# An output product by seven products instead of eight for some pairs of tiles, and gates made in steps

## The chip, the cores and the metric

The kernel runs on one core of one Trainium2 chip. The metric is the device time of one launch in microseconds (us), as the median of several runs. Its engines are named as in the profile: PE multiplies matrices (PEld is its weight load, which runs beside it), DVE and POOL are the vector engines, ACT computes functions, copies and casts, and SP issues the DMAs. Each engine works through its own queue in order, and waits for others by semaphores.

## The reference

Attention of 8 batches, 8 heads, 576 positions and 64 dimensions with two kinds of sparse mask (local for four heads, strided for the others) makes `x`, 4608 tokens by 512. Behind it stands a layer with a gate, which is the part that matters here:

```python
h = x @ w_in            # 4608 x 512 by 512 x 2048
g = h * np.cos(h)       # the gate, elementwise
return (g @ w_out)      # 4608 x 2048 by 2048 x 512
```

Inputs and output are float32 (the weights float64, converted on the chip).

## The kernel before

The program has two stretches. In the first, a loop over slots written out by hand (56 slots for each of the 8 batches, lines 716 to 735) lays the attention of one batch under the input product `x @ w_in` of the one before. That product is made by Strassen's seven products already, with 288 columns to a matmul (line 511), and its result goes to DRAM as `h_all`, 16 tiles ("f tiles") of 128 rows of h by 4608 tokens. In the last batch no attention is left; there `w_out` is read back as float32 (`both`, line 572) and split in two parts for the second stretch, and the first three gates are made.

All products are taken with operands split in two: `split` (line 158) makes a high part by a cast to the type fp32r on ACT (line 159) and a low part as the difference on POOL (line 160). A product is then three matmuls: high by high, high by low, low by high.

The second stretch is the output product `g @ w_out`, lines 739 to 747. It runs over 9 blocks `s` of 512 tokens (`TB`), and in each over the 16 f tiles. For each (s, f), `gate` makes g and `outer` multiplies:

- `gate` (lines 580 to 595) loads 128x512 of h, finds on ACT the whole number of turns k (line 585), subtracts them on DVE (586), takes the sine of the sum with a quarter turn on ACT (587), multiplies by h on DVE (591) and splits (594). The tile `r`, of which there are two, holds k, the rest, the sine and the product in turn; there are four of `g_hi` and `g_lo`. A gate is issued whole, `LAG` = 3 tiles ahead of its use.
- `outer` (lines 597 to 611) runs, for each of four groups of 128 tokens, three matmuls with 128x128 of g as the weight and 128x512 of w_out as the moving operand, into a PSUM bank that collects all 16 f tiles. At the last f tile the bank is copied out, on ACT and DVE in turn, and stored. Eight banks, two for each group, are in use.

The order of instructions on an engine comes from a scheduler that plays the program through with costs of its own. `in_turn` (line 122) keeps the matmuls in the order written, and `with_product` (line 131) keeps an operation from being placed ahead of the matmul that stands before it in the program; neither makes an engine wait.

PSUM has 8 banks; one holds 512 float32 columns. Pools of tiles (`tc.tile_pool`) give out a buffer again once its last reader is done.

Of the kernel before, what the change touches and what calls it, by code (L numbers as in the profile page):

```python
# [25 lines left out]
NTOK = B * S  # L26
P = 128
# [23 lines left out]
NFC = DFF // P  # L51
NF = NFC // 2
# [6 lines left out]
STEP = 7  # L59
# [4 lines left out]
PER_BATCH = NF * STEP  # L64
# [7 lines left out]
PROLOGUE = ((0,), (1,), (2,), (3,), (0, 4), (1, 0, 5), (2, 1, 6), (3, 2), (4, 4), (3,), (5, 5), (6, 6))  # L72
BUSY = (9, 2, 2, 2, 2, 2, 2, 10)

TB = 512
NTB = NTOK // TB
NTT = TB // P
LAG = 3
WG = 3


@with_exitstack
def attention_cos_ffn(ctx, tc, qkl, vl, qkvs, w_in, w_out, eye, eye16, mask_l0, mask_l, mask_s, out):
    nc = tc.nc
# [11 lines left out]
    quarter = const.tile([P, 1], F32, name="quarter")  # L96
# [6 lines left out]
    h_all = dram.tile([NFC, P, NTOK], F32, name="h_all")  # L103
    w_all = dram.tile([NFC, P, DM], F32, name="w_all")
# [26 lines left out]
    def with_product(begun):  # L131
        if turn is not None:
            order(begun, turn, "with this product")
# [21 lines left out]
            out=out, in0=top, scalar=3, in1=bits, op0=ALU.logical_shift_left, op1=ALU.bitwise_or  # L155
        )

    def split(x, hi, lo):
        with_product(nc.scalar.copy(out=hi, in_=x))  # L159
        nc.gpsimd.tensor_tensor(out=lo, in0=x, in1=hi.bitcast(F32), op=ALU.subtract)  # L160

    wi, whole = [], []

# [39 lines left out]
    class Attention:  # L203
        def __init__(self, stack):
            self.plain = True
            self.ld, self.wk = (
                stack.enter_context(tc.tile_pool(name=name, bufs=bufs, side="right", reuse_waits="tile"))
                for name, bufs in (("ld", 3), ("wk", 2))
            )
            self.sm = stack.enter_context(tc.tile_pool(name="sm", bufs=3, side="right"))  # L210
            pn_s.extend(self.wk.tile([P, SU, GP], F32, name=f"pn_s{i}", bufs=1) for i in range(2))
            for t in pn_s:
                nc.gpsimd.memset(t, 0.0)
            self.pn_s = itertools.cycle(pn_s)
            self.kept, self.spare, self.x = None, None, {}
# [349 lines left out]
    def output_weights(n):  # L565
        if n % WG:
            t = wp.tile([P, 2, 2, 2 * P], F32R, name="w", bufs=2 * NF).rearrange("p l m n -> p l (m n)")
        else:
            t = wp.tile([P, 2, 3, 2 * P], F32R, name="v").rearrange("p l m n -> p (l m n)")
            t = t[:, :2 * DM].rearrange("p (l n) -> p l n", l=2)  # L570
        both = more.tile([P, DM], F32, name="both")
# [6 lines left out]
    wo, pend = [], []  # L578

    def gate(s, f):  # L580
        h = hp.tile([P, TB], F32, name="h_in")
        nc.sync.dma_start(out=h, in_=h_all[f, :, s * TB:(s + 1) * TB])
        r = rp.tile([P, TB], F32, name="r")
        k = r.bitcast(I32)
        with_product(nc.scalar.activation(out=k, in_=h, func=AF.Copy, scale=1.0 / (2.0 * math.pi), bias=0.25))  # L585
        nc.vector.scalar_tensor_tensor(out=r, in0=k, scalar=-2.0 * math.pi, in1=h, op0=ALU.mult, op1=ALU.add)  # L586
        sin = nc.scalar.activation(out=r, in_=r, func=AF.Sin, bias=quarter)  # L587
# [3 lines left out]
        nc.vector.tensor_tensor(out=r, in0=r, in1=h, op=ALU.mult)  # L591
        g_hi = gp.tile([P, TB], F32R, name="g_hi")
        g_lo = gp.tile([P, TB], F32R, name="g_lo")
        split(r, g_hi, g_lo)
        return g_hi, g_lo

    def outer(s, f, g_hi, g_lo, acc):
        wh, wl = wo[f]
        for t in range(NTT):
            at = slice(t * P, (t + 1) * P)  # L600
            for i, (g, w) in enumerate(((g_hi, wh), (g_hi, wl), (g_lo, wh))):
                in_turn(nc.tensor.matmul(  # L602
                    acc[t], g[:, at], w, start=(f == 0 and i == 0), stop=(f == NFC - 1 and i == 2)
                ))
            if f == NFC - 1:
                o = op.tile([P, DM], F32, name="o")
                if t % 2:
                    nc.vector.tensor_copy(out=o, in_=acc[t])
                else:
                    nc.scalar.copy(out=o, in_=acc[t])  # L610
                nc.sync.dma_start(out=out[s * TB + t * P:s * TB + (t + 1) * P, :], in_=o)

    wp = ctx.enter_context(tc.tile_pool(name="wp", bufs=NF, reuse_waits="tile"))
    with ExitStack() as phase:
        cv = phase.enter_context(tc.tile_pool(name="cv", bufs=1))
# [8 lines left out]
        pools = banks  # L626
# [7 lines left out]
        m, n, o = ((pools[name], name) for name in "mno")  # L634
        acc = [(ps, f"acc{i}") for i in range(3)]
# [80 lines left out]
        for slot in range(max(plan) + 1):  # L716
            b, at = divmod(slot, PER_BATCH)
            if slot in plan:
                plan[slot]()
            for many, new in bursts.get(slot, ()):  # L720
                burst(many, new)
            for unit in turns.get(slot, ()):
                next(unit)
            for step in steps.get(slot, ()):
                step()
            if b == B - 1:
                if at == 0:
                    attention.close()
# [4 lines left out]
                    more = phase.enter_context(tc.tile_pool(name="more", bufs=WG, side="right", reuse_waits="tile"))  # L733
                if at >= PER_BATCH - 2 * STEP and at % 4 == 0 and len(pend) < LAG:
                    pend.append(gate(0, len(pend)))

    op = ctx.enter_context(tc.tile_pool(name="op", bufs=4, reuse_waits="tile"))
    ps_o = ctx.enter_context(tc.tile_pool(name="ps_o", bufs=2, space=bass.MemoryType.PSUM, reuse_waits="tile"))  # L740
    tiles = [(s, f) for s in range(NTB) for f in range(NFC)]
    for i, (s, f) in enumerate(tiles):
        if f == 0:
            acc = [ps_o.tile([P, DM], F32, name=f"acc{t}") for t in range(NTT)]
        if i + LAG < len(tiles):
            pend.append(gate(*tiles[i + LAG]))
        outer(s, f, *pend.pop(0), acc)


_OUT = ((NTOK, DM), "float32")  # L750
# [92 lines left out]
```

## Time and profile before

| | us |
|---|---|
| median of three runs | 884.25 (882.93 to 885.15) |
| the profiled run | 883.67 |
| its span, first to last instruction | 881.9 |
| input product and attention, up to the first output matmul | about 486 |
| output product, first to last matmul | 391.70 |
| from there to the end | 3.7 |

A row of the groups by line gives line, engine, operation, output and inputs by name, and the shape with the count; then the busy time and the mean of one in ns; then the idle time of the engine just before them, and what ended it. A row of the chain gives start, length and what ran. A row of the windows gives the stretch, its length, for PE, PEld, DVE, ACT and POOL the busy time with the number of instructions, then the granted clock of PE, the DMA share and GB/s. A row of the timeline gives start, length, engine, line, operation and tiles, and in brackets how long the engine was idle before it and who ended that.

### The profile page before, as it was taken

The numbers are of one execution on the slowest core, as the hardware profiler recorded it, in microseconds if no ns is written. First come the engines' busy times: TensorE is split into PE (matmuls) and PEld (weight loads), VectorE is DVE, ScalarE is ACT, GpSimd is POOL, SyncE is SP. The second block draws the span as 40 slices with busy tenths as digits, with TensorE's granted clock in tenths as the row PEclk, the third lists the DMA queues.
The fourth block names the chain that finished last, engine by engine and source line by source line (L and its number), as shares of the span: only waits on it lengthen the run. The fifth ranks groups of instructions, "written<-read, shape, count | busy, mean of one in ns | idle before, by whom it ended". The sixth has DMA issues, their size and how long they took to land.

```text
span 881.9 us, 21351 instructions
## 1 busy us (share of the span) xinstructions
PE 869.3 (99%) x8439; PEld 775.9 (88%) x8439; DVE 562.3 (64%) x966; ACT 530.1 (60%) x1020; POOL 398.2 (45%) x341
## 2 busy tenths in 40 slices
PE   8999999999999999999999999999999999999998
PEld 5799899999999999999999888888888888888886
DVE  5778655767576675676425666666666666666662
ACT  3776544435445463454457777777777777777772
POOL 2578974316024051151355444444444444444442
PEclk9999999999999999999999999999999999999999
DMA  9697444565556556643285434343434344444431
GB/s 333 206 294 259 141 147 158 196 220 191 195 188 234 198 196 201 197 159 122 101 278 188 135 96 144 100 145 101 144 100 141 112 129 120 128 119 121 131 109 48
DMA packets 70516, 143.83 MB, mean 163 GB/s; under 512 B 8208, under 2 KB 15632, under 8 KB 70416
## 3 DMA queue, kind: packets, MB, share of 16 engines
q1 hardware_dynamic: 69696, 142.24, 50.2%
q8 instruction: 66, 1.08, 0.5%
q14 instruction: 34, 0.28, 0.1%
q10 hardware_dynamic: 720, 0.23, 0.1%
HBM read 91.06 MB, written 51.38 MB: 162 GB/s over the span
## 4 chain that ended last, share of the span: by engine, by line
PE 52%; DMA 2%; ACT 1%; POOL 1%; DVE 0%; issue 0%; POOLq 0%; ACTq 0%
PE acc L602 44%; PE m L511 4%; PE n L511 2%; DMA both<-w_all 2%; PE o L511 1%; POOL w L160 1%; PE acc L312 0%; PE acc L377 0%; ACT w L159 0%; ACT r L585 0%; DVE r L586 0%; PE acc L294 0%; ACT r L587 0%; ACT L587 0%; PE acc L364 0%
## 5 line engine op out<-in xcount | busy, mean ns | idle before, releaser
L160 POOL TENSOR_TENSOR g_lo<-r,g_hi 128x512 fp32r<-128x512 f32 x144 | 186.3, 1294 | 205.2 <-ACT g_hi L159 201.0
L602 PE MATMUL acc<-w,g_hi 128*128 128x512 f32 x720 | 221.6, 389 | 0.0
L591 DVE TENSOR_TENSOR r<-r,h_in 128x512 f32<-128x512 f32 x144 | 151.0, 1049 | 103.9 <-ACT r L587 103.6
L602 PEld LDWEIGHTS acc<-w,g_hi 128*128 128x128 f32 x720 | 135.2, 188 | 28.1
L602 PE MATMUL acc<-w,g_lo 128*128 128x512 f32 x360 | 140.0, 389 | 0.0
L585 ACT ACTIVATE r<-h_in 128x512 int32<-128x512 f32 x144 | 91.1, 633 | 77.0 <-POOL g_lo L160 76.3
L602 PE MATMUL acc<-v,g_hi 128*128 128x512 f32 x432 | 133.0, 389 | 0.0
L587 ACT ACTIVATE r<-r,quarter 128x512 f32<-128x512 f32 x144 | 104.4, 725 | 23.1 <-DVE r L586 22.9
L586 DVE SCALAR_TENSOR_TENSOR r<-r,h_in 128x512 f32<-128x512 int32 x144 | 101.7, 707 | 22.4 <-ACT r L585 11.1
L511 PE MATMUL m<-x_hi,w 128*128 128x288 f32 x448 | 109.8, 300 | 1.9 <-DVE h L529 1.5
L511 PE MATMUL m<-x_hi,v 128*128 128x288 f32 x448 | 109.1, 298 | 1.0 <-ACT m L519 0.9
L602 PEld LDWEIGHTS acc<-v,g_hi 128*128 128x128 f32 x432 | 81.0, 188 | 16.8
L159 ACT CAST g_hi<-r 128x512 fp32r<-128x512 f32 x144 | 89.6, 623 | 2.4 <-PE acc L602 1.2
L602 PE MATMUL acc<-v,g_lo 128*128 128x512 f32 x216 | 84.0, 389 | 0.0
L511 PEld LDWEIGHTS m<-x_hi,w 128*128 128x128 f32 x448 | 78.0, 188 | 3.8 <-DVE h L529 2.2
L511 PEld LDWEIGHTS m<-x_hi,v 128*128 128x128 f32 x448 | 78.0, 188 | 2.5 <-ACT m L519 1.7
L602 PEld LDWEIGHTS acc<-w,g_lo 128*128 128x128 f32 x360 | 67.5, 188 | 14.0
L519 ACT COPY m<-m 128x288 f32<-128x288 f32 x112 | 44.5, 397 | 57.3 <-PE m L511 52.3
L511 PE MATMUL m<-x_lo,w 128*128 128x288 f32 x224 | 66.1, 295 | 0.0
L511 PE MATMUL m<-x_lo,v 128*128 128x288 f32 x224 | 66.1, 295 | 0.0
L264 POOL TENSOR_TENSOR pn_s<-e_sb,z 128x324 f32<-128x324 f32 x28 | 21.2, 756 | 93.3 <-DVE z L262 72.2
L264 POOL TENSOR_TENSOR e_sb<-e_sb,z 128x384 f32<-128x384 f32 x24 | 20.9, 872 | 92.1 <-DVE z L262 81.6
(115 smaller groups left out, 1704.5 us busy)
## 6 DMA issues: line engine op xcount, KB each, us to landing
h_all<-h SPq DMA_DIRECT2D x128, 288.0 KB, 2.7
h_in<-h_all SPq DMA_DIRECT2D x144, 256.0 KB, 2.7
out<-o SPq DMA_DIRECT2D x36, 256.0 KB, 2.4
qk<-in_qkvs SPq DMA_DIRECT2D x28, 324.0 KB, 4.0
qk<-in_qkl SPq DMA_DIRECT2D x21, 416.0 KB, 3.9
raw<-in_w_in SPq DMA_DIRECT2D x16, 512.0 KB, 4.7
raw<-in_w_out SPq DMA_DIRECT2D x16, 512.0 KB, 4.3
v<-in_vl SPq DMA_DIRECT2D x24, 224.0 KB, 3.1
```

The lines of the kernel that those rows point to most:

```text
L159: with_product(nc.scalar.copy(out=hi, in_=x))
L160: nc.gpsimd.tensor_tensor(out=lo, in0=x, in1=hi.bitcast(F32), op=ALU.subtract)
L264: nc.gpsimd.tensor_tensor(out=pn, in0=e, in1=z[:, :n].unsqueeze(2).broadcast_to([P, n, w]), op=ALU.mult)
L511: in_turn(nc.tensor.matmul(bank, a[:, c * P:(c + 1) * P], y[:, c], start=first and i == 0, stop=i == len(ops) - 1, skip_group_check=True,))
L519: nc.scalar.copy(out=t, in_=self.bank[name[0]])
L585: with_product(nc.scalar.activation(out=k, in_=h, func=AF.Copy, scale=1.0 / (2.0 * math.pi), bias=0.25))
L586: nc.vector.scalar_tensor_tensor(out=r, in0=k, scalar=-2.0 * math.pi, in1=h, op0=ALU.mult, op1=ALU.add)
L587: sin = nc.scalar.activation(out=r, in_=r, func=AF.Sin, bias=quarter)
L591: nc.vector.tensor_tensor(out=r, in0=r, in1=h, op=ALU.mult)
L602: in_turn(nc.tensor.matmul(acc[t], g[:, at], w, start=(f == 0 and i == 0), stop=(f == NFC - 1 and i == 2)))
```

## The change

The output product now runs over 18 blocks of 256 tokens (`TB = 2 * P`) and in each over 8 pairs of f tiles. A pair is a product of 2 by 2 blocks: two groups of 128 tokens by two f tiles, times two f tiles by two halves (256 columns) of w_out. For the pairs 1, 3 and 5 (`SEVEN`) of the 16 inner blocks it is made by Strassen's seven products, in the form with seven sums on either side; the other pairs, and all pairs of the first and last block, are plain, 12 matmuls of 512 columns as before. A product by seven has 256 columns. Both kinds add into the banks `lower` and `upper` (one for each group of tokens, three in rotation); four quarters of the two banks `more` collect the products that go to more than one place, which DVE adds up (`shared`) and puts on top in `store`.

The gate goes in four steps, issued 6, 4, 3 and 2 pairs ahead (`LEADS`): load; turns and their subtraction; sine and product (with the sums of a seven gate, on POOL); split. The sine goes to a PSUM tile (`wave`, three banks). The sums of w_out for the pairs by seven, and the cast of most of w_out, are made on DVE in the last batch; the last four f tiles of w_out are split in the output product.

```diff
-TB = 512
+TB = 2 * P
 NTB = NTOK // TB
-NTT = TB // P
-LAG = 3
-WG = 3
+SEVEN = (1, 3, 5)
+LEADS = (6, 4, 3, 2)
+AHEAD = tuple(PER_BATCH - n for n in (20, 17, 13, 10, 7, 3))
+BY_VECTOR = (2, 4)
+SUMMED = (14, 28, 35)
+LATE = 4
+OUTPUTS = (
+    (0, "b11", "more", 0), (2, "b21", "upper", 0), (6, "b22", "upper", 1), (1, 3, "lower", 0), (5, 2, "more", 1),
+    (3, 0, "more", 2), (4, 1, "more", 3),
+)
...
-    def split(x, hi, lo):
-        with_product(nc.scalar.copy(out=hi, in_=x))
-        nc.gpsimd.tensor_tensor(out=lo, in0=x, in1=hi.bitcast(F32), op=ALU.subtract)
+    def split(x, hi, lo, cast=nc.scalar.copy, rest=nc.gpsimd):
+        with_product(cast(out=hi, in_=x))
+        rest.tensor_tensor(out=lo, in0=x, in1=hi.bitcast(F32), op=ALU.subtract)
...
-        split(both, t[:, 0], t[:, 1])
+        split(both, t[:, 0], t[:, 1], nc.vector.tensor_copy)
...
+    def output_sums(cv, n):
+        f = SEVEN[n]
+        both = whole_tile(cv).rearrange("p (f n) -> p f n", f=2)
+        nc.sync.dma_start(out=both, in_=w_all[2 * f:2 * f + 2].rearrange("f p n -> p f n"))
...
+        first = nc.vector.tensor_tensor(
+            out=t[:, :2], in0=b[:, 1:2].broadcast_to([P, 2, 2 * P]), in1=b[:, 0:4:3], op=ALU.subtract
+        )
+        nc.vector.tensor_tensor(out=t[:, 2], in0=b[:, 3], in1=t[:, 0], op=ALU.subtract)
+        nc.vector.tensor_tensor(out=t[:, 3], in0=b[:, 2], in1=t[:, 2], op=ALU.subtract)
...
+        split(t[:, :3], most[:, 0], most[:, 1], nc.vector.tensor_copy)
...
+        split(t[:, 3], *last, nc.vector.tensor_copy)
...
     def gate(s, f):
+        h = hp.tile([P, 2 * TB], F32, name="h_in")
+        nc.sync.dma_start(
+            out=h.rearrange("p (f t) -> p f t", f=2),
+            in_=h_all[2 * f:2 * f + 2, :, s * TB:(s + 1) * TB].rearrange("f p t -> p f t"),
+        )
+        yield
...
+        yield
+        wave = sg.tile([P, 2 * TB], F32, name="wave")
+        sin = nc.scalar.activation(out=wave, in_=r, func=AF.Sin, bias=quarter)
...
+        pool = nc.gpsimd
+        if not seven(s, f):
+            low, pool = (wave, nc.vector) if f in BY_VECTOR else (r, nc.gpsimd)
+            nc.vector.tensor_tensor(out=low, in0=wave, in1=h, op=ALU.mult)
+            yield
+            g_hi, g_lo = (gp.tile([P, 7 * P], F32R, name=name) for name in ("g_hi", "g_lo"))
+            split(low, g_hi[:, :4 * P], g_lo[:, :4 * P], rest=pool)
+            gates[s, f] = g_hi, g_lo
+            yield
+        g = gs.tile([P, 8, P], F32, name="g")
+        nc.vector.tensor_tensor(out=g[:, :4].rearrange("p n t -> p (n t)"), in0=wave, in1=h, op=ALU.mult)
+        pool.tensor_tensor(out=g[:, 4], in0=g[:, 0], in1=g[:, 2], op=ALU.add)
+        pool.tensor_tensor(
+            out=g[:, 5:7], in0=g[:, 0:5:4], in1=g[:, 1:2].broadcast_to([P, 2, P]), op=ALU.subtract
+        )
+        pool.tensor_tensor(out=g[:, 7], in0=g[:, 3], in1=g[:, 6], op=ALU.subtract)
+        yield
+        g_hi, g_lo = (gp.tile([P, 7 * P], F32R, name=name) for name in ("g_hi", "g_lo"))
+        split(g[:, 1:].rearrange("p n t -> p (n t)"), g_hi, g_lo)
...
+        def pair(self, f, g_hi, g_lo):
+            (b1h, b1l), (b2h, b2l) = wo[2 * f:2 * f + 2]
+            if not seven(self.s, f):
+                for half, name in enumerate(("lower", "upper")):
+                    for n, (wh, wl) in enumerate(((b1h, b1l), (b2h, b2l))):
+                        gh, gl = (g[:, (2 * n + half) * P:(2 * n + half + 1) * P] for g in (g_hi, g_lo))
+                        self.add(name, 0, 2, ((gh, wh), (gh, wl), (gl, wh)))
+                return
...
+            for n, w, name, at in OUTPUTS:
+                wh, wl = plain[w] if w in plain else sums[f][w]
+                gh, gl = (g[:, n * P:(n + 1) * P] for g in (g_hi, g_lo))
+                self.add(name, at, at + 1, ((gh, wh), (gh, wl), (gl, wh)))
+        def shared(self):
+            more = self.banks["more"]
+            self.t = op.tile([P, 5, 2 * P], F32, name="t")
+            with_product(nc.scalar.copy(out=self.t[:, 0], in_=more[:, 0]))
+            nc.vector.tensor_tensor(out=self.t[:, 4], in0=more[:, 1], in1=self.t[:, 0], op=ALU.add)
+            yield
+            nc.vector.tensor_tensor(
+                out=self.t[:, 1:3], in0=more[:, 2:4], in1=self.t[:, 4:5].broadcast_to([P, 2, 2 * P]), op=ALU.add
+            )
+            nc.vector.tensor_tensor(out=self.t[:, 3], in0=more[:, 2], in1=self.t[:, 2], op=ALU.add)
+            yield
+        def store(self):
...
+                if "more" in self.banks:
+                    nc.vector.tensor_tensor(
+                        out=o, in0=self.banks[name], in1=self.t[:, 2 - 2 * half:4 - 2 * half], op=ALU.add
+                    )
+                elif half:
+                    nc.vector.tensor_copy(out=o, in_=self.banks[name])
+                else:
+                    nc.scalar.copy(out=o, in_=self.banks[name])
...
+                    sg = ctx.enter_context(tc.tile_pool(
+                        name="sg", bufs=3, space=bass.MemoryType.PSUM, side="right", reuse_waits="tile"
+                    ))
-                        for name, bufs in (("gp", LAG + 1), ("hp", 4), ("rp", 2))
+                        for name, bufs in (("gp", 3), ("hp", 5), ("rp", 3))
...
+    gs = ctx.enter_context(tc.tile_pool(name="gs", bufs=3, reuse_waits="tile"))
+    pools = {
+        name: ctx.enter_context(
+            tc.tile_pool(name=f"ps_{bufs}", bufs=bufs, space=bass.MemoryType.PSUM, reuse_waits="tile")
+        ) for name, bufs in (("lower", 3), ("more", 1))
+    }
+    pools["upper"] = pools["lower"]
...
+        ahead(i)
+        for step in made.get(i, ()):
+            next(step, None)
+        block.pair(f, *gates.pop((s, f)))
+        if "more" in block.banks and f >= max(SEVEN):
+            if f == max(SEVEN):
+                shared = block.shared()
+            next(shared, None)
+        if f == NF - 1:
+            block.store()
```

More of the change, by code (lines that the diff above doesn't have):

```diff
@@ L563, in whole_output_weights, with output_weights @@
         yield
[L565 to L571, printed above, removed]
+    def output_weights(both, n):
+        t = wp.tile([P, 2, 2, 2 * P], F32R, name="w", bufs=2 * NF).rearrange("p l m n -> p l (m n)")
@@ new lines, in output_sums @@
+    def output_sums(cv, n):
[3 more added lines that the diff above has]
+        yield
+        b = both.rearrange("p f (j n) -> p (f j) n", j=2)
+        t = whole_tile(cv).rearrange("p (j n) -> p j n", j=4)
+        first = nc.vector.tensor_tensor(
+            out=t[:, :2], in0=b[:, 1:2].broadcast_to([P, 2, 2 * P]), in1=b[:, 0:4:3], op=ALU.subtract
+        )
+        with_product(first)
+        nc.vector.tensor_tensor(out=t[:, 2], in0=b[:, 3], in1=t[:, 0], op=ALU.subtract)
+        nc.vector.tensor_tensor(out=t[:, 3], in0=b[:, 2], in1=t[:, 2], op=ALU.subtract)
+        most = wp.tile([P, 2, 3, 2 * P], F32R, name="v")
+        sums[f] = [(most[:, 0, n], most[:, 1, n]) for n in range(3)]
+        yield
+        split(t[:, :3], most[:, 0], most[:, 1], nc.vector.tensor_copy)
+        yield
+        if n % 3 == 0:
+            lasts.append(wp.tile([P, 2, 3, 2 * P], F32R, name="v"))
+        last = lasts[-1][:, 0, n % 3], lasts[-1][:, 1, n % 3]
+        split(t[:, 3], *last, nc.vector.tensor_copy)
+        sums[f].append(last)
+        yield
@@ L584, in gate, with seven @@
+    wo, lasts, gates, sums = [], [], {}, {}
+    def seven(s, f):
+        return 0 < s < NTB - 1 and f in SEVEN
+    def gate(s, f):
+        h = hp.tile([P, 2 * TB], F32, name="h_in")
[4 more added lines that the diff above has]
+        yield
+        r = rp.tile([P, 2 * TB], F32, name="r")
         k = r.bitcast(I32)
@@ L590, in gate @@
             order(sin, exps[-1], "one change of tables")
[L591 to L601, printed above, removed]
+        pool = nc.gpsimd
@@ new lines, in gate @@
+        pool.tensor_tensor(out=g[:, 4], in0=g[:, 0], in1=g[:, 2], op=ALU.add)
[3 more added lines that the diff above has]
+        pool.tensor_tensor(out=g[:, 7], in0=g[:, 3], in1=g[:, 6], op=ALU.subtract)
+        yield
+        g_hi, g_lo = (gp.tile([P, 7 * P], F32R, name=name) for name in ("g_hi", "g_lo"))
+        split(g[:, 1:].rearrange("p n t -> p (n t)"), g_hi, g_lo)
+        gates[s, f] = g_hi, g_lo
@@ new lines, in gate, with ahead, __init__, add @@
+        yield
+    tiles = [(s, f) for s in range(NTB) for f in range(NF)]
+    work = [gate(*tile) for tile in tiles]
+    def ahead(i):
+        for lead in reversed(LEADS):
+            if 0 <= i + lead < len(work):
+                next(work[i + lead])
+    class Outputs:
+        def __init__(self, s):
+            self.s, self.banks, self.begun = s, {}, set()
+        def add(self, name, begin, end, pairs):
+            if name not in self.banks:
+                n = 4 if name == "more" else 2
+                self.banks[name] = pools[name].tile([P, n, 2 * P], F32, name="q")
+            at = self.banks[name][:, begin:end].rearrange("p n d -> p (n d)")
+            bank = name, begin // 2
+            for a, w in pairs:
@@ L602, in outer @@
                 in_turn(nc.tensor.matmul(
-                    acc[t], g[:, at], w, start=(f == 0 and i == 0), stop=(f == NFC - 1 and i == 2)
+                    at, a, w, start=bank not in self.begun, stop=True, skip_group_check=True
                 ))
[L605 to L608, printed above, removed]
-                else:
-                    nc.scalar.copy(out=o, in_=acc[t])
-                nc.sync.dma_start(out=out[s * TB + t * P:s * TB + (t + 1) * P, :], in_=o)
+                self.begun.add(bank)
@@ new lines, in store @@
+        def store(self):
+            rows = out[self.s * TB:(self.s + 1) * TB, :].rearrange("(h p) d -> h p d", h=2)
+            for half, name in enumerate(("lower", "upper")):
+                o = op.tile([P, 2, 2 * P], F32, name="o", bufs=4)
+                if "more" in self.banks:
[4 more added lines that the diff above has]
+                    nc.vector.tensor_copy(out=o, in_=self.banks[name])
+                else:
+                    nc.scalar.copy(out=o, in_=self.banks[name])
+                nc.sync.dma_start(out=rows[half], in_=o.rearrange("p n d -> p (n d)"))
@@ L715, in attention_cos_ffn @@
                 steps.setdefault(at + made, []).append(partial(lambda b, i: operands[b].make(i), b, i))
-        for slot in range(max(plan) + 1):
+        for slot in range(max(*plan, *steps) + 1):
             b, at = divmod(slot, PER_BATCH)
@@ L732, in attention_cos_ffn @@
                     )
[L733 to L741, printed above, removed]
+                if at in AHEAD:
+                    ahead(AHEAD.index(at) - len(AHEAD))
@@ new lines, in attention_cos_ffn @@
+    op = ctx.enter_context(tc.tile_pool(name="op", bufs=2, reuse_waits="tile"))
+    tp = ctx.enter_context(tc.tile_pool(name="tp", bufs=1, reuse_waits="tile"))
+    gs = ctx.enter_context(tc.tile_pool(name="gs", bufs=3, reuse_waits="tile"))
[5 more added lines that the diff above has]
+    pools["upper"] = pools["lower"]
+    made = {}
@@ L742, in attention_cos_ffn @@
+    for n in range(NFC - LATE, NFC):
+        weights = output_weights(tp.tile([P, DM], F32, name=f"both{n}"), n)
+        next(weights)
+        made[n + LATE - NFC + 1] = [weights]
     for i, (s, f) in enumerate(tiles):
         if f == 0:
[L744 to L747, printed above, removed]
+            block = Outputs(s)
+        ahead(i)
[8 more added lines that the diff above has]
+            block.store()
```

22 lines of the change are left out of this document (14 added, 8 removed).

## The prediction

> **What bounds the kernel now.** I read the page first, for the busy shares, then the chain that ended last in order of time, then the windows, and then the groups by line with shapes apart.
>
> ```profile
> span 881.9 us, 21351 instructions
> PE 869.3 (99%) x8439; PEld 775.9 (88%) x8439; DVE 562.3 (64%) x966; ACT 530.1 (60%) x1020; POOL 398.2 (45%) x341
> ```
> ```profile
> 387.70 0.33 PE acc L364 x3
> ...
> 397.74 1.60 PE m L511 x12
> ...
> 485.44 1.06 PE m L511 x6
> 486.50 391.70 PE acc L602 x1728
> 878.22 0.69 DVE o L608
> ```
> ```profile
> 440.00:481.00 41.00, 41.00 (x310) 40.97 (x308) 13.83 (x26) 24.86 (x53) 24.49 (x19) 1.00 0.74 238
> ```
> ```profile
> 486.50:878.20 391.70, 391.68 (x1728) 323.98 (x1727) 255.49 (x298) 282.06 (x441) 182.46 (x141) 1.00 0.40 116
> ```
>
> The reader is to see one piece of 391.70 us: the output product, 1728 matmuls without a hole, at a granted clock of 1.00. That is 226.7 ns for each matmul of 512 columns. In that piece DVE is busy 255 us, ACT 282 and POOL 182, so PE sets the end there. But the gates are not far behind:
>
> ```profile
> POOL g_lo L160 <- ACT g_hi L159: 196.8, 138, 3.2
> ACT r L585 <- POOL g_lo L160: 76.3, 131, 0.8
> POOL g_lo L160 <- PE acc L602: 4.2, 3, 1.4
> ```
>
> These waits (total, times, longest) say that the engines that make the gates wait for one another, almost never for PE: the gate chain of before runs only just ahead of its 12 matmuls (2.72 us). A faster PE needs a faster chain.
>
> **The change, part by part.**
>
> *The matmuls.* Before, 256 tokens and two f tiles cost 12 matmuls of 512 columns; a plain pair still does. A pair by seven products costs 7 x 3 = 21 matmuls of 256 columns. There are 18 x 8 = 144 pairs, of which 16 x 3 = 48 are done by seven, so 96 x 12 = 1152 matmuls of 512 and 48 x 21 = 1008 of 256 replace the 1728. The trace has no 256-column matmul. From 288 columns (12 in 1.60 us, 133.3 ns each) to 512 (226.7 ns) a column costs 0.417 ns, and 13.3 ns do not depend on the columns: 120.0 ns at 256. From above the 288-column row bounds it, 133.3 ns. From below the three transposes of 128 columns, 0.33 us or 110 ns each; by the line 128 columns would take 67, so something other than the columns, the weight load as far as the trace shows, sets those 110. I take 120: it lies on the line through the two shapes of the same operands, and 288 is the nearest row. Then the product takes 1152 x 0.2267 + 1008 x 0.1200 = 261.2 + 121.0 = 382.1 us, which is **9.6 less**: 0.20 for each pair by seven (2.72 to 2.52), 0.6 for each of the 16 inner blocks.
>
> The Trainium skill, "TensorE: Matmul & The Clock Gate", section "Back-to-back issue gap", gives a warm gap of columns / 2.4 plus 2.5 ns: 215.8 at 512 and 109.2 at 256, as an estimate, and the product would save 14 us from such a base. The trace does not agree at 512 (226.7 measured), so the measurement decides, and the 110 stays as a rival.
>
> *What feeds them.* An inner block has five plain pairs and three by seven: PE 5 x 2.72 + 3 x 2.52 = 21.16 us. The rows for the rest:
>
> ```profile
> L585 ACT ACTIVATE r<-h_in 128x512 int32<-128x512 f32 x144 | 91.1, 633 | 77.0 <-POOL g_lo L160 76.3
> L587 ACT ACTIVATE r<-r,quarter 128x512 f32<-128x512 f32 x144 | 104.4, 725 | 23.1 <-DVE r L586 22.9
> L159 ACT CAST g_hi<-r 128x512 fp32r<-128x512 f32 x144 | 89.6, 623 | 2.4 <-PE acc L602 1.2 <-DVE r L591 1.0 <-issue 0.2
> L159 ACT CAST v<-sums 128x768 fp32r<-128x768 f32 x8 | 6.7, 836 | 2.8 <-POOL w L160 1.5 <-POOL sums L192 1.4
> L610 ACT COPY o<-acc 128x512 f32<-128x512 f32 x18 | 10.3, 571 | 9.0 <-PE acc L602 9.0
> L519 ACT COPY m<-m 128x288 f32<-128x288 f32 x112 | 44.5, 397 | 57.3 <-PE m L511 52.3 <-ACT x_hi L159 1.9 <-issue 1.1
> L586 DVE SCALAR_TENSOR_TENSOR r<-r,h_in 128x512 f32<-128x512 int32 x144 | 101.7, 707 | 22.4 <-ACT r L585 11.1
> L591 DVE TENSOR_TENSOR r<-r,h_in 128x512 f32<-128x512 f32 x144 | 151.0, 1049 | 103.9 <-ACT r L587 103.6
> L529 DVE TENSOR_TENSOR h<-n,m 128x288 f32<-128x288 f32 x56 | 25.3, 451 | 37.0 <-PE n L511 33.1 <-ACT e_sb L258 3.6
> L255 DVE TENSOR_TENSOR acc<-acc,ml 128x384 f32<-128x384 f32 x21 | 11.8, 562 | 12.1 <-PE acc L294 12.1
> L160 POOL TENSOR_TENSOR g_lo<-r,g_hi 128x512 fp32r<-128x512 f32 x144 | 186.3, 1294 | 205.2 <-ACT g_hi L159 201.0 <-PE acc L602 4.2
> L160 POOL TENSOR_TENSOR v<-sums,v 128x768 fp32r<-128x768 f32 x8 | 14.8, 1849 | 6.4 <-ACT v L159 6.4
> L187 POOL TENSOR_TENSOR v<-v 128x256 f32<-128x256 f32 x8 | 5.9, 739 | 0.2
> ```
>
> A gate tile still holds 128x512 elements (two f tiles of 256 tokens). ACT does range (0.633) and sine (0.725) eight times, five casts of 512 (0.623), three of 896 columns (836 plus 128 x 0.83 = 0.942) and one copy of at most 0.40: 10.86 + 3.12 + 2.83 + 0.40 = 17.2 us. That the sine now writes PSUM has no row; between the 0.57 of a PSUM copy (L610) and a tenth more than 0.725 the sum stays under 18. DVE: the product of sine and h has one operand in PSUM. Rows L529 and L255, both with a PSUM operand, give 451 at 288 and 562 at 384 columns, so 0.71 at 512 and 0.41 at 256, against 1.049 from SBUF. Eight products, two subtractions for the pairs in BY_VECTOR, two stores and one shared sum of 512 make 13 x 0.71; two of 256 make 0.83; eight range reductions 5.66: 15.7 us. POOL: 2.17 ns a column between 512 and 768, so 896 take 2.13 and 128 take 0.46. A seven gate costs 0.46 + 0.74 + 0.46 + 2.13 = 3.79; three of them and three plain ones of 1.294 make 15.2 us.
>
> All are under 21.16, so the first answer is that they hide. But two of them cannot run together:
>
> ```profile
> 477.88 1.28 POOL L160 TENSOR_TENSOR g_lo<-r,g_hi 128x512 fp32r<-128x512 f32 x1
> 477.98 1.73 DVE L586 SCALAR_TENSOR_TENSOR r<-r,h_in 128x512 f32<-128x512 int32 x1 [1.22 <-ACT r L585]
> ```
>
> The range reduction began 0.10 after POOL, ended 0.55 after POOL's end, and took 1.73 for its 0.69: with both operands in SBUF it waits POOL out. POOL's 15.2 plus 8 x 0.55 is 19.6 of 21.16 us, 93%. That is the tightest cover of the change. I cost it at nothing, because a gate's sines and sums are issued three pairs ahead and its split two pairs ahead; how it can fail is the first rival.
>
> *New waits.* The three banks that lower and upper share: the second half of the next block's first pair waits for the store of this block's lower half. From the last matmul into lower to that reuse lie 12 matmuls, 2.72 us; the store takes 0.71 and at worst a range reduction of 1.73 stands before it on DVE: 2.44, covered by 0.3. More has one buffer but four pairs between its reading and its next use. On SP, h comes in runs half as long:
>
> ```profile
> h_in<-h_all SPq DMA_DIRECT2D x144, 256.0 KB, 2.7
> ```
>
> Loads go out six pairs ahead and are used two pairs (5.2 us) later; even twice 2.7 would miss by only 0.2, with DMA at a share of 0.40. Nothing is charged.
>
> *The last batch.* Twelve splits move their cast from ACT to DVE, three sums with two casts each are new on DVE, and four splits move into the output product, where pair 0 to 5 don't need them. DVE was busy 13.8 of 41 us; twelve casts at about 0.7 (the range reduction's row) and three sums at about 3 (1.5 for the sums themselves, as much for their casts) add some 17 us, so it is busy 3/4 of the time, and the additions that free PE's banks stand in the same queue. What a late one costs:
>
> ```profile
> 485.43 0.19 PEld L511 LDWEIGHTS m<-x_hi,w 128*128 128x128 f32 x1 [0.79 <-DVE h L529]
> ```
>
> Bounds: 15 pieces x 0.79 = 12 us above; below, the 0.8 us hole goes as ACT is relieved. Nearest is the one hole of this size, so I take **+1.0**. The Trainium skill, "SBUF — State Buffer", section "Who interferes with whom", adds that a copy or cast on VectorE in a two-port mode locks GpSimd out; no row here shows such a cast.
>
> *The end.* The last block is plain; its last DVE copy and DMA stay as they are: 0.
>
> **Sum.** 883.67 (profiled run; 881.9 of span and 1.8 around it) - 9.6 + 1.0 = 875.1. The median shown, 884.25, is 0.6 above the profiled run: **875.7 us**.
>
> **Rivals.**
>
> *The seven gates come late (slower).* ACT works in order. Say cast j+2 stands before sine j+3. The sums of a seven gate end about 0.62 + 0.73 + 0.71 + 1.66 = 3.7 us after its pair slot begins, 1.0 into the next slot, 1.6 if a range reduction takes its 0.55 between them. ACT then waits, and sine and product of the next tile are late by as much; each further seven gate, two slots later, adds 0.8, or 1.35 with the 0.55. The third (pair 5) has its sums 2.6 to 4.3 into the slot, its low part 0.94 + 2.13 later, at 5.7 to 7.4, and PE wants it at 5.24 + 0.24 = 5.5: late by 0.2 to 1.9 us in each of 16 blocks, 3 to 30 us. At the middle, 1.05 x 16 = 16.8, the time is 892.5; it decides from 0.6 us per block. What speaks for it, beside the waits above, is the order that before ran in:
>
> ```profile
> 523.13 0.62 ACT L159 CAST g_hi<-r 128x512 fp32r<-128x512 f32 x1
> 523.92 0.72 ACT L587 ACTIVATE r<-r,quarter 128x512 f32<-128x512 f32 x1 [0.17 <-DVE r L586]
> 525.21 0.63 ACT L585 ACTIVATE r<-h_in 128x512 int32<-128x512 f32 x1 [0.56 <-POOL g_lo L160]
> 525.81 0.62 ACT L159 CAST g_hi<-r 128x512 fp32r<-128x512 f32 x1
> ```
>
> The cast of one tile, the sine of the next, its range, its cast: a loop of 2.68 us with ACT idle in it twice. Against: if sines are queued before a cast whose sums aren't there, the split ends at 4.4 and PE waits for nothing, and before had only two buffers for r where three stages now have three.
>
> *The weight load limits 256 columns at the 133 ns of 288 (slower).* PEld's share is 88%. Then a pair takes 21 x 0.1333 = 2.80, 0.08 more than plain: + 3.8 + 1.0, 889.1 us. It turns at 129.5 ns. Against: 288 and 512 lie on one line of 2.4 columns per ns, which a weight limit at 288 would only meet by accident.
>
> *256 columns go at the transposes' 110 ns (faster).* 48 x (2.72 - 2.31) = 19.7 less, plus 1.0: 865.6 us. The page's rule gives the same 109; against it, both rows of this type carry 13.3 ns.
>
> *DVE stalls the last batch.* Up to 12 instead of 1: 886.7.
>
> **How the numbers follow.** Forecast 0.52 (872 to 879: 119 to 121 ns, -0.8 to +3 at the start). Late gates 0.30: of that 0.03 still faster, 0.08 within, 0.19 slower. Weight load 0.08 (0.06 slower, 0.02 within, since it can lie between). 110 ns 0.07. Last batch 0.03 (0.02 within, 0.01 slower). Faster by over 0.3% (what a measurement here can tell from no change, 2.7 us): 0.62; within 0.12; slower 0.26. Below 870 lies most of the 110 ns case, 0.06; above 893 about half of the late gates that are slower and the far end of their bounds, 0.12. So 870 to 893.
>
> **What would show it.** Matmuls of 256 in steps of 0.12 us, and 21 of them in 2.52: right; 0.133: the weight load. The chain of waits after the last batch as one piece of PE, near 382 us: right; with pieces of POOL g_lo and waits of PE for it at pairs 1, 3 and 5 of inner blocks: the late gates. Waits of PE on the additions to h between 440 and 487 us beyond 2 us would make the start term wrong, and products of sine and h that take 1 us instead of 0.71 would take away the cover on DVE.

## The result, and the profile after

The changed kernel takes 892.47 us in the median of four runs (890.62 to 893.41), the kernel before 884.35: a ratio of 1.0091, 95% interval 1.0069 to 1.0113. It is slower by 0.9%, where 875.7 was forecast. The page of the profiled run (893.41 us, the slowest of the four):

```profile
span 891.6 us, 22375 instructions
PE 867.6 (97%) x8871; PEld 788.7 (88%) x8871; DVE 611.6 (69%) x1097; ACT 506.3 (57%) x1004; POOL 516.3 (58%) x455
```

PE is busy 1.7 us less and the span is 9.7 longer, so PE now waits. The list of PE's waits in the whole trace (total, times, longest) says on whom:

```profile
PE q L681 <- DVE o L721: 8.1, 15, 1.2
PE m L524 <- DVE h L542: 2.6, 4, 1.5
```

The first row is new: in the inner blocks PE waits for the store (L721), once a block. The matmuls themselves do what was forecast. The timeline of PE in one block boundary, and behind it the first pair by seven:

```profile
644.84 0.62 PE L681 MATMUL q<-w,g_hi 128*128 128x512 f32 x2
645.29 0.39 PE L681 MATMUL q<-w,g_lo 128*128 128x512 f32 x1
646.20 0.74 PE L681 MATMUL q<-w,g_hi 128*128 128x512 f32 x2 [0.52 <-DVE o L721]
...
648.42 0.40 PE L681 MATMUL q<-w,g_hi 128*128 128x256 f32 x2
648.66 0.28 PE L681 MATMUL q<-w,g_lo 128*128 128x256 f32 x1
648.78 0.40 PE L681 MATMUL q<-v,g_hi 128*128 128x256 f32 x2
```

Three matmuls of 256 columns start in 648.42 to 648.78, 0.120 us each, as the line through 288 and 512 columns gave. But from 645.29 to 646.20, from one matmul's start to the next, 0.91 us pass instead of 0.23: the one that comes late is the seventh of the new block's first pair, the first into the bank that the old block's lower half leaves. With the slower restart after it this block loses 0.79 us. Blocks follow each other every 22.04 us (this wait ends at 624.16 and at 646.20), where 21.16 were worked out.

Over the whole trace the span grew by 9.7 us in four places, by the start of the first matmul of each stretch, which the timeline gives: 2.2 before the last batch, in code that nothing was changed in (the traces of the ten variants below, with the same code there, begin their last batch at 438.8 to 440.4 us, before at 440.25, and this trace alone at 442.5, so this part is not the change's); 2.5 in the last batch (46.1 to 48.6 us); 4.8 in the output product (391.5 to 396.3); 0.2 behind it. The product's 4.8 is 9.6 saved and 14.4 given back, 13.0 of it as waits like the one shown, counted by the starts of the matmuls (the list above has 8.1, since a part of each is the weight load's wait and the slow restart), and most of the rest as told in the last section.

What stands in front of the store is in DVE's and POOL's timelines of the same boundary:

```profile
640.63 1.56 DVE L631 SCALAR_TENSOR_TENSOR r<-r,h_in 128x512 f32<-128x512 int32 x2
642.11 0.41 DVE L707 TENSOR_TENSOR t<-q,t 128x256 f32<-128x256 f32 x1
642.56 0.69 DVE L709 TENSOR_TENSOR t<-q,t 128x512 f32<-128x512 f32 x1
643.17 0.69 DVE L641 TENSOR_TENSOR wave<-wave,h_in 128x512 f32<-128x512 f32 x1
643.76 0.68 DVE L648 TENSOR_TENSOR g<-wave,h_in 128x512 f32<-128x512 f32 x1
644.36 0.41 DVE L712 TENSOR_TENSOR t<-q,t 128x256 f32<-128x256 f32 x1
644.69 0.85 DVE L631 SCALAR_TENSOR_TENSOR r<-r,h_in 128x512 f32<-128x512 int32 x1
645.46 1.28 DVE L721 TENSOR_TENSOR o<-q,t 128x512 f32<-128x512 f32 x2
```
```profile
640.73 0.91 POOL L649 TENSOR_TENSOR g<-g 128x128 f32<-128x128 f32 x1 [0.37 <-DVE g L648]
641.72 1.07 POOL L650 TENSOR_TENSOR g<-g 128x256 f32<-128x256 f32 x1
642.75 1.30 POOL L173 TENSOR_TENSOR g_lo<-r,g_hi 128x512 fp32r<-128x512 f32 x1
644.00 0.46 POOL L653 TENSOR_TENSOR g<-g 128x128 f32<-128x128 f32 x1
```

DVE has no idle gap from 640.63 to the store at 645.46: eight operations run through, and the store is the ninth. POOL's 128x128 sum at 640.73 takes 0.91, a sum of the same shape at 644.00 only 0.46; the first ran beside the range reductions (L631), the second did not. The groups by line, with shapes apart, from 520 to 860 us give the means of the output product:

```profile
L631 DVE SCALAR_TENSOR_TENSOR r<-r,h_in 128x512 f32<-128x512 int32 x124 | 125.2, 1030 | 6.4 <-ACT r L630 6.4
L641 DVE TENSOR_TENSOR r<-wave,h_in 128x512 f32<-128x512 f32 x48 | 32.9, 686 | 36.8 <-ACT wave L634 36.8
```
```profile
L173 POOL TENSOR_TENSOR g_lo<-g,g_hi 128x896 fp32r<-128x896 f32 x47 | 100.0, 2127 | 41.7 <-ACT g_hi L172 41.7
L173 POOL TENSOR_TENSOR g_lo<-r,g_hi 128x512 fp32r<-128x512 f32 x47 | 68.2, 1451 | 20.0 <-ACT g_hi L172 20.0
L650 POOL TENSOR_TENSOR g<-g 128x256 f32<-128x256 f32 x46 | 44.3, 963 | 2.4
L649 POOL TENSOR_TENSOR g<-g 128x128 f32<-128x128 f32 x46 | 35.2, 764 | 6.4 <-DVE g L648 5.6
```

The sizes of single operations came out as worked out where the other engine was not in the way: 0.69 for the product of sine and h (0.71 forecast), 2.13 for the long subtraction. Where DVE and POOL meet, both grow: the range reduction 0.71 to 1.03, POOL's sums 0.46 to 0.76 and 0.74 to 0.96, its short subtraction 1.29 to 1.45. And two rows of the waits in the same stretch:

```profile
ACT g_hi L172 <- POOL g L653: 66.2, 46, 2.2
POOL g_lo L173 <- ACT g_hi L172: 61.7, 63, 1.3
```

ACT's casts wait for POOL's sums 46 times, once for each seven gate in the stretch, and POOL's subtractions wait for the casts, 61.7 us or 4.0 a block. In the kernel before the casts of the gates waited 2.4 us in all.

### The profile page after: what moved, and what is told of

Same layout as the page of the kernel before. It is cut to its first block, busy times and chain, and to the rows that moved or that the text cites. A ratio compares the mean times of both kernels' runs of the same rounds, so it can differ in the third digit from the quotient of the medians.

```text
span 891.6 us, 22375 instructions
## 1 busy us (share of the span) xinstructions
PE 867.6 (97%) x8871; PEld 788.7 (88%) x8871; DVE 611.6 (69%) x1097; ACT 506.3 (57%) x1004; POOL 516.3 (58%) x455
## 3 DMA queue, kind: packets, MB, share of 16 engines
q8 instruction: 69, 1.13, 0.5%
## 4 chain that ended last, share of the span: by engine, by line
PE 37%; DVE 9%; issue 4%; ACT 3%; POOL 3%; POOLq 0%; DVEq 0%
PE q L681 28%; PE m L524 5%; DVE r L631 3%; POOL g_lo L173 3%; PE n L524 3%; ACT r L630 2%; PE o L524 1%; DVE t L709 1%; DVE o L721 1%; ACT wave L634 1%; DVE g L648 1%; DVE t L707 1%; DVE t L712 1%; DVE h L542 0%; PE acc L325 0%
## 5 line engine op out<-in xcount | busy, mean ns | idle before, releaser
L681 PE MATMUL q<-w,g_hi 128*128 128x512 f32 (+1 forms) x1056 | 293.4, 363 | 8.1 <-DVE o L721 8.1
L681 PEld LDWEIGHTS q<-w,g_hi 128*128 128x128 f32 x1056 | 187.6, 189 | 44.9 <-DVE o L721 14.8
L681 PE MATMUL q<-w,g_lo 128*128 128x512 f32 (+1 forms) x528 | 190.3, 360 | 0.0
L631 DVE SCALAR_TENSOR_TENSOR r<-r,h_in 128x512 f32<-128x512 int32 x144 | 144.0, 1019 | 9.8 <-ACT r L630 9.8
L173 POOL TENSOR_TENSOR g_lo<-g,g_hi 128x896 fp32r<-128x896 f32 x48 | 102.1, 2127 | 41.7 <-ACT g_hi L172 41.7
L634 ACT ACTIVATE wave<-r,quarter 128x512 f32<-128x512 f32 x144 | 98.2, 690 | 40.0 <-DVE r L631 40.0
L681 PEld LDWEIGHTS q<-w,g_lo 128*128 128x128 f32 x528 | 99.5, 188 | 15.8 <-POOL g_lo L173 0.2
L173 POOL TENSOR_TENSOR g_lo<-r,g_hi 128x512 fp32r<-128x512 f32 x60 | 85.8, 1431 | 35.8 <-ACT g_hi L172 34.5
L172 ACT CAST g_hi<-g 128x896 fp32r<-128x896 f32 x48 | 45.3, 944 | 68.8 <-POOL g L653 68.8
L277 POOL TENSOR_TENSOR pn_s<-e_sb,z 128x324 f32<-128x324 f32 x28 | 21.2, 758 | 94.1 <-DVE z L275 76.3
L681 PE MATMUL q<-v,g_hi 128*128 128x256 f32 x384 | 71.2, 283 | 0.0
```

Of the source, the lines that this page charges most:

```text
L172: with_product(cast(out=hi, in_=x))
L173: rest.tensor_tensor(out=lo, in0=x, in1=hi.bitcast(F32), op=ALU.subtract)
L277: nc.gpsimd.tensor_tensor(out=pn, in0=e, in1=z[:, :n].unsqueeze(2).broadcast_to([P, n, w]), op=ALU.mult)
L634: sin = nc.scalar.activation(out=wave, in_=r, func=AF.Sin, bias=quarter)
L681: in_turn(nc.tensor.matmul(at, a, w, start=bank not in self.begun, stop=True, skip_group_check=True))
```

## The experiments

Theory A: PE loses at one place alone, the reused bank, because the store stands late in DVE's queue; a fourth bank mends it. Theory B: the gates cannot be made faster than 22.0 us a block, because POOL and the range reduction wait for each other, and the bank is only where that shows. The texts call this sharing a port: the runs show the waiting, and that it goes with a second operand in SBUF. Theory C concerns the last batch: PE waits for additions to h behind casts on DVE that wait for POOL. Each time is a median of at least four runs, and each ratio, with its 95% interval, is to runs of the kernel before on the same chip.

**Four banks.**

```diff
-                        name="sg", bufs=3, space=bass.MemoryType.PSUM, side="right", reuse_waits="tile"
+                        name="sg", bufs=2, space=bass.MemoryType.PSUM, side="right", reuse_waits="tile"
...
-        ) for name, bufs in (("lower", 3), ("more", 1))
+        ) for name, bufs in (("lower", 4), ("more", 1))
```

> Four buffers instead of three for the banks lower and upper, and two instead of three for the sine in PSUM. Theory A (in each inner block PE loses 0.8 us at one place alone: its first matmul into the reused bank waits for the store of the block before, which stands late in DVE's queue): with a fourth bank that wait goes, blocks take 21.2 us instead of 22.0, the time falls by about 12 to 879 to 882. Theory B (the gates cannot be made faster than 22.0 us a block, because POOL and the range reduction share a port, and the bank is only where it shows): blocks stay at 21.9 to 22.1, PE waits for gates instead, 890 to 893. Two sine tiles may also hold the gates back, which would look like B with ACT's sine waiting for DVE.

It took 891.82 us, 1.0092 (1.0075 to 1.0109): no gain. The wait has moved. PE's waits in the whole trace, then the shares of the chain that ended last between 640 and 690 us:

```profile
PE q L681 <- POOL g_lo L173: 7.7, 14, 0.6
```
```profile
by line: POOL g_lo L173 44.0%; POOL g L650 17.6%; ACT g_hi L172 9.5%; POOL g L649 7.2%; issue 6.7%; POOL g L653 6.3%; ACT wave L634 2.8%; DVE g L648 2.8%; DVE r L631 2.8%; ACT r L630 2.6%; POOLq L173 0.3%
```

With the bank out of the way, PE waits once a block for the low part of pair 1, and the chain runs through POOL for 75% of the time (44.0 + 17.6 + 7.2 + 6.3) and through the casts that POOL waits for. The product takes 396.2 us, the changed kernel's 396.3. Theory A alone is out. Two sine tiles did not hold ACT: the sine still waits only for the range reduction.

**All pairs plain.**

```diff
-SEVEN = (1, 3, 5)
+SEVEN = ()
...
-SUMMED = (14, 28, 35)
+SUMMED = ()
```

> No pair by seven and no sums of the output weights: all 144 pairs plain, everything else as in the changed kernel. Both theories: PE 12 x 0.2267 a pair, 391.7 us for the product, and no sums in the stores. Theory A: no wait at the bank, so 21.8 us a block; with about 1 us lost in the last batch 884 to 887, so the pairs by seven lose 6 us net as they stand. If other parts of the change (steps, 256 tokens, sine in PSUM) cost as well, 889 or more.

883.81 us, 1.0003 (0.9993 to 1.0012). The product takes 391.5 us without a wait, and its range reductions 0.689. So steps, 256 tokens and the sine in PSUM cost nothing that shows in the time; the eight microseconds come with the pairs by seven and their sums. The last batch takes 46.6 us here, although twelve casts of w_out are still on DVE.

**Casts of the weights back on ACT.**

```diff
-        split(both, t[:, 0], t[:, 1], nc.vector.tensor_copy)
+        split(both, t[:, 0], t[:, 1])
...
-        split(t[:, :3], most[:, 0], most[:, 1], nc.vector.tensor_copy)
+        split(t[:, :3], most[:, 0], most[:, 1])
...
-        split(t[:, 3], *last, nc.vector.tensor_copy)
+        split(t[:, 3], *last)
```

> The casts of the output weights and of their sums back on ACT, as before the change. Theory C (in the last batch PE waits for the additions to h because casts stand before them on DVE and wait for POOL to end): the waits of PE in that batch fall from 3.8 us to about 1.3, the time by about 2.4, to 889 to 890.5. Rival: the sums and range reductions on DVE do it, or ACT then frees its banks late: 892 to 893. The blocks of the output product stay at 22.0.

888.86 us, 1.0052 (1.0037 to 1.0067), about 3.4 less than the changed kernel by the ratios, with some 2 us of doubt by the intervals. The last batch takes 46.9 us instead of 48.6, and PE waits 1.0 us in it instead of 2.7; the output product takes 396.3 as ever. The rows that say why are the changed kernel's: on DVE's timeline in the last batch, then DVE and POOL together at its end, then PE:

```profile
476.74 0.42 DVE L172 CAST w<-raw 128x512 fp32r<-128x512 f32 x1
```
```profile
487.35 1.74 POOL L173 TENSOR_TENSOR g_lo<-r,g_hi 128x512 fp32r<-128x512 f32 x1
487.86 1.51 DVE L172 CAST w<-raw 128x512 fp32r<-128x512 f32 x1
489.30 0.44 DVE L542 TENSOR_TENSOR h<-n,m 128x288 f32<-128x288 f32 x1
```
```profile
490.16 0.40 PE L524 MATMUL m<-x_hi,w 128*128 128x288 f32 x1 [1.49 <-DVE h L542]
```

A cast of 512 columns takes 0.42 us alone and 1.51 where POOL's subtraction runs; it ends 0.28 after POOL does. The two additions to h stand behind it, and PE waits 1.49 for them. Theory C holds for this wait, the longest of three. The casts do it only together with the sums: with all pairs plain the casts are on DVE without the sums, and here the sums without the casts, and either way the batch takes less than 47 us.

**The turns in PSUM.**

```diff
         r = rp.tile([P, 2 * TB], F32, name="r")
-        k = r.bitcast(I32)
+        wave = sg.tile([P, 2 * TB], F32, name="wave")
+        k = wave.bitcast(I32)
...
-        wave = sg.tile([P, 2 * TB], F32, name="wave")
```

> The turns k go to the PSUM tile that the sine takes later, so that the range reduction on DVE has one operand in SBUF instead of two. It should take 0.69 us each time instead of 1.02 on the mean. Theory A: DVE comes to the store earlier by up to 2.6 us a block, the wait at the bank falls from 0.8 to between 0 and 0.3, 879 to 885. Theory B: POOL is freed of the port as well, so the same or more. If the three sine tiles, now held one step longer, hold ACT back: no gain, 890 to 895, with ACT waiting for DVE before the range.

876.90 us, 0.9914 (0.9899 to 0.9928): faster than both kernels, and a little below what either theory gave. The output product takes 383.6 us, 12.7 less than the changed kernel's. Groups by line from 520 to 860 us, then the waits there:

```profile
L632 DVE SCALAR_TENSOR_TENSOR r<-wave,h_in 128x512 f32<-128x512 int32 x128 | 85.9, 682 | 1.6
```
```profile
L173 POOL TENSOR_TENSOR g_lo<-r,g_hi 128x512 fp32r<-128x512 f32 x51 | 66.2, 1298 | 39.7 <-ACT g_hi L172 39.2
L650 POOL TENSOR_TENSOR g<-g 128x256 f32<-128x256 f32 x45 | 33.5, 743 | 1.2
L649 POOL TENSOR_TENSOR g<-g 128x128 f32<-128x128 f32 x45 | 21.0, 466 | 20.7 <-DVE g L648 20.7
```
```profile
ACT g_hi L172 <- PE q L681: 87.9, 96, 1.4
```

With one SBUF operand in the range reduction, both sides are at the durations that the prediction took from the trace of before: 0.68, 1.30, 0.74, 0.47. And the casts now wait for PE, 96 times: the gates are ahead, held only by their buffers, and PE never waits in this stretch. The windows 580 to 668, four blocks of the changed kernel, set the two kernels side by side (the changed one first; PE, PEld, DVE, ACT, POOL):

```profile
580.00:668.00 88.00, 86.12 (x492) 74.93 (x492) 66.33 (x93) 60.54 (x101) 69.48 (x61) 1.00 0.40 120
```
```profile
580.00:668.00 88.00, 88.00 (x515) 78.13 (x513) 57.70 (x96) 62.35 (x104) 62.13 (x63) 1.00 0.41 124
```

**The turns in tiles of their own in SBUF.** With k in PSUM two things changed: one SBUF operand less, and `r` no longer held from the turns on. This run changes the second and keeps two operands in SBUF; k has two buffers here, where the PSUM tile has three.

```diff
-        r = rp.tile([P, 2 * TB], F32, name="r")
-        k = r.bitcast(I32)
+        k = rp.tile([P, 2 * TB], I32, name="k", bufs=2)
...
+        r = rp.tile([P, 2 * TB], F32, name="r")
         nc.vector.scalar_tensor_tensor(out=r, in0=k, scalar=-2.0 * math.pi, in1=h, op0=ALU.mult, op1=ALU.add)
```

> The turns k get two tiles of their own in SBUF, and r is taken only by the range reduction, as it was with k in PSUM; but the range reduction keeps two operands in SBUF. It tells the two things apart that the kernel with k in PSUM changed at once. If the port that the range reduction shares with POOL was the cause (theory B), it still takes 1.0 us and the blocks stay at about 22.0: 889 to 893. If the tile r, held from the turns to the split, was the cause, the time falls as it did with k in PSUM, to 876 to 879.

910.55 us, 1.0311 (1.0295 to 1.0327): neither 877 nor 890, but 18 us above the changed kernel. Two rows, of the groups and of the waits from 520 to 860 us:

```profile
L631 DVE SCALAR_TENSOR_TENSOR r<-k,h_in 128x512 f32<-128x512 int32 x117 | 130.2, 1132 | 0.0
```
```profile
POOL g L649 <- DVE g L648: 35.0, 30, 2.1
```

The range reduction meets POOL still more (1.13), and now POOL also waits for the product behind it (35.0 us; 5.6 in the changed kernel). So freeing `r` is not what helped, and two SBUF operands are enough to keep the loss. Nor is it the order of the queues: in the traces POOL runs each block in the same order here and with k in PSUM, and the orders of DVE and of ACT differ in one exchange of neighbours each. ACT's waits from 520 to 860 us are for POOL's sums, the range reduction and PE (78.2, 38.1 and 1.1 us), none for a buffer of k. What is left between 910.55 and 876.90 us is the place of one operand. Why this kernel loses so much more than the changed one, whose order differs a little more, is not settled. One cause can be seen: a range reduction that starts at 642.24, 0.03 after a subtraction on POOL, takes 1.81, and POOL then stands idle for 2.08 until the product behind it is there; how much of the 18 us this makes was not counted.

**The turns in PSUM and the casts on ACT.** Both edits above together.

> k in PSUM and the casts of the output weights back on ACT. If the two losses, port and last batch, are independent, the waits of PE in the last batch go from 2.6 us to about 1.5 to 2, blocks stay at 21.16, and the time is 874 to 876. If ACT is late with its banks instead, 876.9 as with k in PSUM alone.

875.00 us, 0.9904 (0.9890 to 0.9919), the lowest median here, though the intervals don't part it from k in PSUM alone. The last batch takes 46.6 us (47.3 with k in PSUM alone); the chain ends in one piece:

```profile
485.58 383.06 PE q L681 x2160
```

**Four pairs by seven**, with k in PSUM.

```diff
-SEVEN = (1, 3, 5)
+SEVEN = (1, 3, 5, 6)
...
-SUMMED = (14, 28, 35)
+SUMMED = (14, 28, 35, 42)
```

> k in PSUM and a fourth pair (6) by seven in the inner blocks. POOL has 4 x 3.79 + 2 x 1.29 = 17.7 us of work in a block of 4 x 2.72 + 4 x 2.52 = 20.96. If POOL's work hides without the port conflict, the product loses another 16 x 0.2 = 3.2 us, and with one more sum in the last batch the time is 873.5 to 875. If two pairs by seven in a row make the gates late, PE waits for POOL at pair 6 or 7, by up to 1 us a block, and the time is 877 to 890.

876.66 us, 0.9927 (0.9910 to 0.9944): as with three, and between the two ranges. The fourth pair saves its 3.2 us, and PE loses 3.7 us at three places, two in the first block, which is plain (up to 498.8 and 502.9 us), and one at the start of the last (849.6). In between no matmul waits.

**Two pairs by seven**, k in SBUF as in the changed kernel.

```diff
-SEVEN = (1, 3, 5)
+SEVEN = (1, 5)
...
-SUMMED = (14, 28, 35)
+SUMMED = (14, 35)
```

> The changed kernel with two pairs by seven (1 and 5) instead of three. POOL has 2 x 3.79 + 4 x 1.29 = 12.8 us in a block of 6 x 2.72 + 2 x 2.52 = 21.36, and with 8 x 0.55 of range reductions 17.2 for the shared port, instead of 19.6 of 21.16. Theory B: the gates are in time, no wait at the bank, the product is 6.4 us shorter than before, and with 2 us lost in the last batch the time is 878 to 881. If the wait at the bank came from the store and the shared sums alone, which stay, blocks lose 0.5 to 0.8 as before: 887 to 893.

881.16 us, 0.9973 (0.9960 to 0.9986). The rows of the range reduction and of one of POOL's sums from 520 to 860 us, and a row of ACT's waits:

```profile
L631 DVE SCALAR_TENSOR_TENSOR r<-r,h_in 128x512 f32<-128x512 int32 x127 | 93.5, 755 | 50.0 <-ACT r L630 50.0
```
```profile
L650 POOL TENSOR_TENSOR g<-g 128x256 f32<-128x256 f32 x30 | 32.2, 1074 | 2.4
```
```profile
ACT g_hi L172 <- PE q L681: 61.2, 79, 1.1
```

Store, shared sums and banks are the same as with three pairs, and from 520 us on there is no wait at the bank (one of 1.3 us comes before). The two engines still meet, but now POOL pays most of it: the reduction takes 0.755 on the mean, POOL's sums 0.88 and 1.07, more than in the changed kernel. With one seven gate less POOL has time for that (58.90 of 88 us busy instead of 69.48), and the casts wait for PE: the gates are ahead.

**Pair 7's subtraction on DVE too.** It takes work from POOL and gives it to the engine that the store waits on, with three pairs by seven and k in SBUF.

```diff
-BY_VECTOR = (2, 4)
+BY_VECTOR = (2, 4, 7)
```

> The changed kernel with the subtraction of pair 7 on DVE too (BY_VECTOR of 2, 4 and 7): POOL has one operation of 1.3 to 1.45 us less in a block, DVE one of 0.69 more. If POOL's chain, lengthened by the port, sets the 22.0 us of a block (POOL busy 17.4 of it), blocks come down by most of 0.8, to 21.2 to 21.5: 879 to 885. If DVE's queue ahead of the store sets it, the wait at the bank grows by up to 0.69 a block: 893 to 904.

882.01 us, 0.9982 (0.9971 to 0.9993), about 10 less than the changed kernel. Four blocks, in the windows:

```profile
580.00:668.00 88.00, 87.84 (x504) 76.74 (x504) 73.15 (x98) 61.51 (x103) 66.07 (x58) 1.00 0.40 121
```

DVE is busier than in the changed kernel (73.15 to 66.33) and yet the blocks are shorter, 21.6 us. What is left of the wait is still at the bank, 0.3 a block. So it is POOL's chain that sets the pace, not the length of DVE's queue.

**Four pairs, k in PSUM, casts on ACT.**

> k in PSUM, the casts of the output weights on ACT, and four pairs by seven. The four pairs saved 3.2 us in the product and lost it again in the first inner block; the casts on ACT take DVE out of POOL's way in the last batch. If both last: 874.8, and if the first inner block's waits of 2.4 us come from what the last batch left behind, 872.5. If ACT is late in the last batch: 877.

875.60 us, 0.9907 (0.9890 to 0.9925), the same as with three pairs. The waits of the first block are still 1.7 us (2.4 with the casts on DVE), so most of them does not come from what DVE's casts left behind; where they come from was not tried.

## Why the prediction was wrong

The forecast failed in one step, the cover of POOL's work, and lost a smaller sum in a second, the last batch.

*The matmuls: right.* 120.0 ns at 256 columns was forecast and 120 is what the rows show. From first to last start the output product fell from 391.46 us to 382.82 in the kernel that has no wait there: 8.6 of the 9.6 forecast. The Trainium skill, "TensorE: Matmul & The Clock Gate", section "Back-to-back issue gap", would give 109.2 ns, as an estimate. The trace does not agree (120.0), as at 512 columns.

*What feeds them: this step failed.* The text had the port ("it waits POOL out"), the sum of 19.6 of 21.16 us, and then the words "I cost it at nothing". Two things were wrong in that. First, 0.55 was added for each range reduction, and nothing for what POOL waits in its turn. The runs show that both wait: the reduction grows by 0.32 and POOL's operations by up to 0.30 each, so POOL is busy 17.4 us of a block (69.48 in four) and DVE 16.6 (66.33), where 15.2 and 15.7 were worked out. Second, a share of 93% was read as cover. POOL's operations are not one queue of work that can be taken in any order: a seven gate goes sine, product, three operations for the sums (four sums of g, not seven as the description of the change has it), cast on ACT, subtraction, and POOL stands still for the casts, 4.0 us a block. 17.4 us of work, these 4.0 and a few tenths for the product make up nearly all of the 22.0, and PE follows. Taking the port away (k in PSUM) or 1.3 us of POOL's work (pair 7 on DVE) or a seven gate (two pairs) each brought the blocks back to 21.2 to 21.6; a fourth bank and a shorter hold on `r` did not.

*The new wait: wrong, but not the cause.* "Covered by 0.3" allowed for one range reduction ahead of the store. Eight operations stood there, among them the sums L709 and L712, which the store needs and which the text had in DVE's total alone. The wait was exactly there, 0.79 us in the block shown. The run with four banks shows that closing it gives nothing, as long as POOL's chain is what is late.

*The last batch: mis-sized.* 1.0 was charged and 2.5 measured in the profiled run; the three other traces with the casts and three sums on DVE and k in SBUF give 2.6 to 3.0. PE waits 2.7 us on the additions to h, over the 2 that the prediction had named as the sign. What the term left out is that the new work on DVE and POOL's subtractions wait for one another: a cast takes 0.42 us alone and 1.51 beside POOL, with the additions behind it. The Trainium skill, "SBUF — State Buffer", section "Who interferes with whom", has a cast on VectorE in a two-port mode and GpSimd exclude one another. The trace agrees; in this case it was the cast that waited. The prediction had named that sentence and given it no cost.

*The rivals.* "The seven gates come late" named the mechanism. That its middle, 892.5, is what was measured is luck: in the profiled run the product gave back 14.4 us where that rival had 16.8, the last batch lost 2.5 where it had 1.0, and 2.2 came ahead of it. Its order was there too:

```profile
627.23 0.94 ACT L172 CAST g_hi<-g 128x896 fp32r<-128x896 f32 x1 [2.18 <-POOL g L653]
628.07 0.69 ACT L634 ACTIVATE wave<-r,quarter 128x512 f32<-128x512 f32 x1
```

The cast waits 2.18 us for the sums, with the next sine behind it. Its place was wrong: PE stops at the reused bank at a block's start, not at pairs 1, 3 and 5. And the order alone does no harm: with k in PSUM the long cast still stands before a sine, it waits only 9.9 us for POOL's sums in the stretch instead of 66.2, and PE does not wait. Its chance, 0.30 against 0.52, looks low afterwards: the loop in the profile of before was only 0.04 us shorter than PE's 2.72. The other rivals didn't occur: the matmuls of 256 columns took neither 133 nor 110 ns, and the last batch lost 2.5 us, not 12.

## What to carry to other kernels

When operations of two engines cannot run together, add their work as one resource, and then ask what each waits for the other and for the steps between. By the prediction's own sum 17.2 of 21.36 us (81%, two pairs by seven) hid here, 18.3 of 21.16 (86%, pair 7 on DVE) still lost 0.4 us a block, and 19.6 (93%) lost 0.9; another order of the queues lost more. Read which operands lie where: moving one operand of one operation to PSUM gave 12.7 us in the output product, more than the 9.6 that the change was to save. And where PE waits is not always where the time is lost: free that wait in an experiment, and see whether it only moves.

## What the hardware showed that was not expected

The matmuls of 512 columns right behind a pair by seven are longer. In the kernel with k in PSUM and the casts on ACT, PE's timeline:

```profile
602.44 0.28 PE L681 MATMUL q<-v,g_lo 128*128 128x256 f32 x1
602.56 0.63 PE L681 MATMUL q<-w,g_hi 128*128 128x512 f32 x2
603.02 0.39 PE L681 MATMUL q<-w,g_lo 128*128 128x512 f32 x1
603.25 0.63 PE L681 MATMUL q<-w,g_hi 128*128 128x512 f32 x2
603.72 0.39 PE L681 MATMUL q<-w,g_lo 128*128 128x512 f32 x1
603.94 0.62 PE L681 MATMUL q<-w,g_hi 128*128 128x512 f32 x2
```

From 602.56 to 603.94 six of them take 1.38 us instead of 6 x 0.2267 = 1.36, and over all blocks of that run the first five are longer by 27 ns together, 1.3 us in the product, of which the first matmul of 256 columns of a pair, 6 ns shorter than the others, gives 0.3 back. That is the 1.0 us by which the product missed its forecast. With 256 columns the weight load may be so near its limit that it needs five longer matmuls to come ahead again; no run tested that.
